# Products of k and v head by head in column tiles of 64, and loads issued at other steps of a span

## Chip, cores and metric

The kernel runs on one core of a Trainium2 chip. The metric is the device time of the whole launch in microseconds (us); the median of several runs is compared. The core has five engines that are told apart below: TensorE (PE, whose weight loads the profile lists apart as PEld), VectorE (DVE), ScalarE (ACT), GpSimd (POOL) and SyncE (SP). In this kernel POOL and SP mostly issue transfers, each through a queue of its own that is worked off in order.

## What is computed

Linear attention feeds a gated two-layer network. There are 8 batches, 8 heads, 576 positions and 64 dimensions per head, so 4608 tokens of width 512; the hidden width is 1536.

```python
q_s = exp(q - max(q, -1)); q_s /= sum(q_s, -1) + 1e-9
k_s = exp(k - max(k, 2));  k_s /= sum(k_s, 2) + 1e-9     # softmax over the positions
kv = einsum('bhsd,bhse->bhde', k_s, v)                   # 64 x 64 for each batch and head
x = einsum('bhsd,bhde->bhse', q_s, kv)                   # then (tokens, 512)
out = (sigmoid(x @ w_gate) * (x @ w_val)) @ w_out
```

## The kernel before

**Tiling.** Tokens are worked in nine windows of 512. Window 0 runs while the weights arrive and are prepared (the loop over j from 0 to 11, functions g1_0 and g2_0). From window 1 on each window is one span of six steps, at = 0 to 5, each over 256 of the 1536 hidden columns. A step is g1 (84 matmul passes, L696), h_split, side_a, g2 of the step before (48 passes, L768) and side_b. side_a(n, at) and side_b(n, at) prepare window n = w + 1 and batch n while window w multiplies: they are the attention part, cut into pieces p = 0 to 5 that go with the six steps.

**Products of k and v (k_mm, L381 to L392).** The 576 positions of a batch are five tiles: four of 128 rows and one of 64. Two heads (a pair, hp) stand side by side in 128 columns. For each tile and pair one matmul takes 128 columns of k as weights and 128 columns of v as the moving operand, so it computes four 64x64 blocks; the two on the diagonal are the two heads' products, the other two are not used. A batch has 20 matmuls into one PSUM tile named at. The data are float32, which TensorE works in two passes, so the profile shows 40 weight loads and 40 matmul records per batch. They are the step p = 2 of a span for batches 2 to 7, between g1 and g2; for batch 1 they stand in the first loop at j = 5, and batch 0 has a form of its own (k_mm_0).

**After the products (k_done, L410).** DVE scales the two diagonal blocks by the reciprocal sums with one instruction for each half of the partitions (diag_put, L398) into kmax_b, and kv_split makes a high and a low part for the second product (x_mm, L560).

**Loads (load_next, L839).** While window n is prepared, load_next(n, p) issues on SP what batch n + 1 needs: kT (k transposed, tiles kt, two 288 KB loads at p = 1 and two at p = 3), and at p = 5 four q tiles (ring<-qn_in), five k tiles (ring<-k_in) and five v tiles (v and f_last), 256 KB each, the last of k and v 128 KB. It stands at the end of side_b. Other SP transfers of a span are the maxima and sums of q to DRAM and back (q_m_row, q_r_row, then eight spread loads each into q_b, L491), q transposed (ring<-qT_in, L498) at p = 1, and the results (out). The four combined weights of the next step (s_sb, L288, 512 KB each) and the second-layer weights (wo_hl, L238) are reloaded in every step on POOL's queue; a reload is issued when the matmuls that read the tile are done, and the tile is read again one step later.

Of the kernel before, what the change touches and what calls it, by code (L numbers as in the profile page):

```python
# [8 lines left out]
F32 = mybir.dt.float32  # L9
# [5 lines left out]
ALU = mybir.AluOpType  # L15
AX = mybir.AxisListType

P = 128
B, H, S, D = 8, 8, 576, 64
# [6 lines left out]
NP = H // 2  # L26
# [4 lines left out]
NC = 4  # L31
# [20 lines left out]
def attn_moe(ctx: ExitStack, tc: tile.TileContext, qf, qn, qT, k, kT, v, wg, wv, wo, out):  # L52
    nc = tc.nc
# [23 lines left out]
    ps_at = ctx.enter_context(tc.tile_pool(name="ps_at", bufs=1, space=bass.MemoryType.PSUM))  # L77
# [14 lines left out]
        out=kv_sb.rearrange("p b i h e -> p (b i h e)"),  # L92
# [204 lines left out]
    kvps = {}  # L297
# [6 lines left out]
    def kT_load(b, hp, t=None):  # L304
        if t is None:
            t = kt_two[hp % 2]
            nc.sync.dma_start(out=t, in_=kT[b, hp * P:(hp + 1) * P])
        kT_sb[b, hp] = t

    def k_max(b, hp):  # L310
        if hp == 0:
            kmax[b], kneg[b], ksum[b] = (
                small.tile([P, NP], F32, name=f"k_{x}") for x in ("max", "neg", "sum")
            )
        m = kmax[b][:, hp:hp + 1]
        nc.vector.tensor_reduce(out=m, in_=kT_sb[b, hp], axis=AX.X, op=ALU.max)
        nc.vector.tensor_scalar(
            out=kneg[b][:, hp:hp + 1], in0=m, scalar1=-1.0, scalar2=None, op0=ALU.mult
        )

    def k_sum(b, hp):
        t = kT_sb.pop((b, hp))
        nc.scalar.activation(
            t, t, AF.Exp, bias=kneg[b][:, hp:hp + 1], accum_out=ksum[b][:, hp:hp + 1]
        )
# [11 lines left out]
    def k_load(b, t, kt=None):  # L337
        s0, n = KTILES[t]
        if kt is None:
            kt = ring.tile([P, DM], F32, name="ring")  # L340
        nc.sync.dma_start(out=kt[:n], in_=k[b, s0:s0 + n])
        kt_sb[b, t] = kt

    def v_load(b, t, vt=None):
        s0, n = KTILES[t]
        if vt is None:

            if t < 2:
                vt = v_two[t]
            else:  # L350
                vt = f_last[:, t - 2].rearrange("p n e -> p (n e)")
        v_sb[b, t] = vt
        src = v[b, s0:s0 + n]
        if b == 0:
            nc.sync.dma_start(out=vt[:n, :, 0:P], in_=src.rearrange("s (h e) -> s h e", e=P))
        else:
            nc.sync.dma_start(out=vt[:n], in_=src)
# [23 lines left out]
    def k_mm(b, t):  # L381
        n = KTILES[t][1]
        kt, vt = kt_sb[b, t], v_sb[b, t]
        if t == 0:
            kvps[b] = ps_at.tile([P, NP, P], F32, name="at")
        for hp in range(NP):
            sl = slice(hp * P, (hp + 1) * P)
            nc.tensor.matmul(  # L388
                kvps[b][:, hp], lhsT=kt[:n, sl], rhs=vt[:n, sl],
                start=(t == 0 and hp == 0), stop=(t == len(KTILES) - 1 and hp == NP - 1),  # L390
                skip_group_check=True,
            )  # L392

    def diag_put(o, ps, k_r, h0, h1):

        for a in range(2):
            sl = slice(a * D, (a + 1) * D)
            nc.vector.tensor_tensor(  # L398
                out=o(sl), in0=ps[sl, :, sl],
                in1=k_r[sl, h0:h1].unsqueeze(2).broadcast_to([D, h1 - h0, D]), op=ALU.mult,  # L400
            )
# [8 lines left out]
    def k_done(b):  # L410
        k_r = ksum.pop(b)
        nc.vector.tensor_scalar_add(k_r, k_r, EPS)
        nc.vector.reciprocal(k_r, k_r)
        kv = kmax_b[:, 0:NP * D].rearrange("p (h e) -> p h e", e=D)
        diag_put(lambda sl: kv[sl], kvps.pop(b), k_r, 0, NP)
        kv_32[b] = lambda sl: kv[sl]

    kv_32 = {}
# [24 lines left out]
    def qn_load(w, c):  # L443
        t = ring.tile([P, T], F32, name="ring")
        nc.sync.dma_start(out=t, in_=qf[w, c] if w < NF else qn[w - NF, c])
        qn_sb[w, c] = t.rearrange("p (i d) -> p i d", d=D)
# [41 lines left out]
    def q_spread(w, what, hp):  # L488
        q_b[w, what, hp] = t = four.tile([P, T], F32, name="q_b")
        for a in range(2):  # L490
            nc.sync.dma_start(  # L491
                out=t[a * D:(a + 1) * D],
                in_=q_row[w, what][2 * hp + a].unsqueeze(0).broadcast_to([D, T]),
            )

    def qT_load(w, hp):
        qT_sb[w, hp] = t = ring.tile([P, T], F32, name="ring")
        nc.sync.dma_start(out=t, in_=qT[w - NF, hp])  # L498
# [20 lines left out]
    def qT_mul(w, hp, eng=nc.vector):  # L519
        t = qT_sb[w, hp]  # L520
        eng.tensor_tensor(out=t, in0=t, in1=q_b.pop((w, "r", hp)), op=ALU.mult)
# [19 lines left out]
    def x_mm(w, hp):  # L541
        qh, ql = qT_hl.pop((w, hp))
        if w > 1 and hp < 3:
            ps = ps_gv.tile([P, T], F32, name="gv")
        else:
            ps = ps_at.tile([P, T], F32, name="at")
        x_ps[w, hp] = ps
        parts = x_parts(w)
        if len(parts) == 1 and hp == NP - 1:
            parts = [(parts[0][0], f, f + HT) for f in range(0, T, HT)]  # L550
        if w > 1 and hp == NP - 1:
            parts.sort(key=lambda x: (P <= x[2] - x[1] <= HT, x[2] - x[1]))
        for b, f, t in parts:
            kh, kl = (kv_sb[:, b % 2, i, hp] for i in range(2))
            for lh, rh in ((0, qh), (0, ql), (1, qh)):
                cuts = [f, t]
                if w > 1 and hp == NP - 1 and lh and t == parts[-1][2] and t - f > HT:
                    cuts.insert(1, (f + t) // 2)
                for f0, t0 in zip(cuts, cuts[1:]):
                    nc.tensor.matmul(  # L560
                        ps[:, f0:t0], lhsT=kl if lh else kh, rhs=rh[:, f0:t0],
                        start=(lh == 0 and rh is qh), stop=(lh == 1),
                        skip_group_check=True,
                    )

    def x_ev(w, hp):
        copy = nc.vector.tensor_copy if hp % 2 and w > 1 else nc.scalar.copy
        copy(out=x_32[:, hp], in_=x_ps.pop((w, hp)))
# [30 lines left out]
    def c_subs():  # L599

        def sub(i, x, y):
            c_32[i] = t = ring.tile([P, 2, HT], F32, name="ring")
            nc.vector.tensor_tensor(out=t, in0=x, in1=y, op=ALU.subtract)

        sub(T1, quarter(0, 1), quarter(0, 0))
        sub(T2, quarter(1, 1), c_32[T1])
        sub(T3, quarter(1, 1), quarter(0, 1))
        sub(T4, quarter(1, 0), c_32[T2])
# [209 lines left out]

    def side_b(n, p):
        if p == 0:  # L820
            for hp in range(NP):
                q_spread(n, "m", hp)
        if p == 1:
            for hp in range(NP):
                qT_load(n, hp)
        if p == 2:
            for hp in range(NP):
                q_spread(n, "r", hp)
        if p == 3:
            for hp in range(NP):  # L830
                qT_mul(n, hp)
        if p == 4:
            for hp in range(NP):
                x_mm(n, hp)
                x_ev(n, hp)
            c_subs()
        load_next(n, p)

    def load_next(n, p, vs=range(5)):  # L839

        if n + 1 >= NW:
            return
        b = n + 1 if n + 1 < B else None
        if b is not None:
            if p == 1:
                kT_load(b, 0); kT_load(b, 1)
            if p == 2:
                k_max(b, 0); k_max(b, 1)
            if p == 3:
                k_sum(b, 0); k_sum(b, 1)  # L850
                kT_load(b, 2); kT_load(b, 3)
            if p == 4:
                k_max(b, 2); k_max(b, 3)
                k_max_send(b)
                if b > 2:
                    k_max_read(b)
        if p == 5:
            for c in range(NC):
                qn_load(n + 1, c)
            if b is not None:  # L860
                for t in range(5):
                    k_load(b, t)
                for t in vs:
                    v_load(b, t)

# [71 lines left out]
    for t in range(0, 4, 2):  # L939
        rows = k[0, t * P:(t + 2) * P].rearrange("(t p) e -> p t e", p=P)  # L940
# [14 lines left out]
    for g in range(2):  # L955
        rows = kT[1, 2 * g * P:2 * (g + 1) * P].rearrange("(g p) s -> p g s", p=P)
# [23 lines left out]
    for t in range(2, 5):  # L980
        n = KTILES[t][1]
        nc.vector.tensor_tensor(out=top[:n], in0=top[:n], in1=kt_sb[0, t][:n], op=ALU.max)
    ps = ps_acc.tile([P, DM], F32, name="acc")
    for hp in range(NP):
# [6 lines left out]
        out=m, in_=ps.rearrange("p (h s) -> p h s", s=P), axis=AX.X, op=ALU.max  # L991
    )
    nc.vector.tensor_tensor(
        out=diag.rearrange("p (h s) -> p h s", s=P),
        in0=ident.unsqueeze(1).broadcast_to([P, NP, P]),
        in1=m.broadcast_to([P, NP, P]), op=ALU.mult,
# [105 lines left out]
    j, p = NJ - 1, NS - 1  # L1102
# [25 lines left out]
    for w in range(1, NW):  # L1128
        last = w == NW - 1
        for at in range(NS):  # L1130
            p = step(w, at)
# [61 lines left out]
```

## Time and profile before

| | |
|---|---|
| runs | 948.31, 948.54, 952.85 us; median 948.54 |
| profiled execution | 952.18 us, of which the profile's span is 950.2 us |
| PE busy in the span | 931.5 us, 7218 matmul records |
| DVE, ACT, POOL busy | 614.2, 487.7, 176.4 us |
| mean granted TensorE clock | 0.990 of 2.4 GHz |
| moved by DMA | 257.94 MB, mean 271 GB/s |

Busy time alone doesn't say what bounds the end: matmuls are pipelined, so PE counts as busy when it waits between two passes too. The rows further down are read by the distance between starts and by the waits.

### The profile page before, as it was taken

Reading aid. Unit: us, or ns where it says so; the run is one execution under the profiler, and the core shown is the slowest. Engines: PE = TensorE matmul, PEld = TensorE weight load, DVE = VectorE, ACT = ScalarE, POOL = GpSimd, SP = SyncE. Lnnn points to the kernel's source line nnn. Section 1 sums busy time; section 2 is a strip of 40 time slices with the busy share of each in tenths; the row PEclk is TensorE's granted clock in tenths of the full one; section 3 lists DMA queues with packets and bytes.
Section 4 is the critical chain, followed back from the end, with each engine's and each line's share of the span. In section 5 each row is a group of like instructions: output and inputs, shape, how many; then the busy total and the mean of one; then the engine's idle time right before and its main releaser. Section 6 shows DMA issues by size and latency. Waiting matters only on the chain.

```text
span 950.2 us, 18015 instructions
## 1 busy us (share of the span) xinstructions
PE 931.5 (98%) x7218; PEld 853.9 (90%) x7218; DVE 614.2 (65%) x1014; ACT 487.7 (51%) x824; POOL 176.4 (19%) x334
## 2 busy tenths in 40 slices
PE   5999899999999999999999999999999999999998
PEld 4644544799999999999999999999999999999998
DVE  7698879876566666656675668466755755564242
ACT  4589887564456345635472647264635343543222
POOL 0110112321122112211221222121212122212220
PEclk8899999999999999999999999999999999999999
DMA  9967686999699979998899979997999689858672
GB/s 315 346 221 287 217 299 199 365 361 298 206 264 361 295 233 249 371 293 270 210 379 301 275 167 382 325 285 153 382 321 260 213 248 324 249 179 264 204 218 69
DMA packets 96610, 257.94 MB, mean 271 GB/s; under 512 B 15568, under 2 KB 18128, under 8 KB 96528
## 3 DMA queue, kind: packets, MB, share of 16 engines
q0 software_dynamic: 46304, 168.32, 58.6%
q1 hardware_dynamic: 50224, 88.48, 32.1%
q8 instruction: 57, 0.93, 0.4%
q14 instruction: 25, 0.20, 0.1%
HBM read 228.20 MB, written 28.56 MB: 270 GB/s over the span
## 4 chain that ended last, share of the span: by engine, by line
PE 82%; issue 8%; DVE 4%; DMA 2%; POOL 1%; ACT 1%; SPq 0%; POOLq 0%; ACTq 0%; DVEq 0%
PE gv L696 48%; PE acc L768 28%; PE at L388 3%; PE gv L560 2%; DMA wo_raw<-wo_in 1%; POOL s L281 1%; DMA s<-s_sb 1%; DMA lent<-k_in 1%; PE at L560 1%; DVE s_sb L276 1%; DVE a_w L276 0%; POOL wo L229 0%; DVE c_hl L624 0%; PE acc L584 0%; PE gv L644 0%
## 5 line engine op out<-in xcount | busy, mean ns | idle before, releaser
L696 PE MATMUL gv<-c_hl,s_sb 128*128 128x256 f32 x2304 | 277.2, 276 | 0.0
L768 PE MATMUL acc<-wo_hl,h 128*128 128x256 f32 x2304 | 269.5, 276 | 0.0
L696 PEld LDWEIGHTS gv<-c_hl,s_sb 128*128 128x128 f32 x2304 | 268.6, 188 | 0.1
L768 PEld LDWEIGHTS acc<-wo_hl,h 128*128 128x128 f32 x2304 | 264.7, 188 | 0.7
L696 PE MATMUL gv<-c_hl,a_w 128*128 128x256 f32 x1728 | 220.6, 277 | 0.7 <-DVE h L656 0.7
L696 PEld LDWEIGHTS gv<-c_hl,a_w 128*128 128x128 f32 x1728 | 206.9, 188 | 1.8 <-DVE h L656 0.9
L288 POOL DMA_DIRECT2D s_sb<-s x188 | 99.6, 530 | 302.3 <-PE gv L696 300.3
L722 DVE TENSOR_TENSOR sg<-gv,sg 128x512 f32<-128x512 f32 x48 | 33.2, 691 | 134.7 <-PE gv L696 134.5
L238 POOL DMA_DIRECT2D wo_hl<-wo x96 | 50.9, 530 | 295.6 <-PE acc L768 293.2
L714 ACT COPY sg<-gv 128x512 f32<-128x512 f32 x48 | 28.2, 588 | 143.7 <-PE gv L696 143.0
L724 ACT COPY sg<-gv 128x512 f32<-128x512 f32 x48 | 28.2, 587 | 103.3 <-PE gv L696 103.3
L644 PE MATMUL gv<-x,f_w 128*128 128x512 f32 x160 | 72.2, 605 | 2.8 <-DVE h L656 2.8
L726 DVE TENSOR_TENSOR sg<-sg 128x512 f32<-128x512 f32 x48 | 33.2, 692 | 53.9 <-ACT sg L724 53.9
L644 PEld LDWEIGHTS gv<-x,f_w 128*128 128x128 f32 x160 | 30.6, 194 | 40.5 <-issue 35.8
L747 DVE TENSOR_TENSOR h<-sg,h 128x1024 fp32r<-128x1024 f32 x48 | 58.8, 1226 | 1.6
L735 DVE TENSOR_TENSOR sg<-sg 128x512 f32<-128x512 f32 x48 | 33.2, 692 | 33.6 <-ACT sg L729 33.6
L729 ACT ACTIVATE sg<-sg 128x512 f32<-128x512 f32 x48 | 30.4, 634 | 46.2 <-DVE sg L728 46.2
L719 ACT COPY sg<-gv 128x512 f32<-128x512 f32 x48 | 28.2, 587 | 37.2 <-PE gv L696 37.2
L716 ACT COPY sg<-gv 128x512 f32<-128x512 f32 x48 | 28.2, 587 | 36.7 <-PE gv L696 36.7
L678 PE MATMUL acc<-wo_t,h 128*128 128x512 f32 x96 | 43.1, 592 | 0.0
L502 DVE TENSOR_TENSOR ring<-ring,q_b 128x512 f32<-128x512 f32 x28 | 18.5, 691 | 37.8 <-DMA ring<-qT_in 37.6
L678 PEld LDWEIGHTS acc<-wo_t,h 128*128 128x128 f32 x96 | 18.2, 190 | 22.7 <-issue 21.3
(154 smaller groups left out, 1066.6 us busy)
## 6 DMA issues: line engine op xcount, KB each, us to landing
s_sb<-s POOLq DMA_DIRECT2D x188, 512.0 KB, 8.1
wo_hl<-wo POOLq DMA_DIRECT2D x96, 512.0 KB, 6.4
s<-s_sb POOLq DMA_DIRECT2D x24, 512.0 KB, 5.6
out<-x SPq DMA_DIRECT2D x35, 256.0 KB, 9.6
ring<-k_in SPq DMA_DIRECT2D x28, 256.0 KB, 14.7
ring<-qn_in SPq DMA_DIRECT2D x28, 256.0 KB, 10.4
q_b<-q_m_row SPq DMA_DIRECT2D x56, 128.0 KB, 9.7
ring<-qT_in SPq DMA_DIRECT2D x28, 256.0 KB, 6.9
```

The source lines that it names most:

```text
L238: nc.gpsimd.dma_start(out=t.rearrange("p h e -> p (h e)"), in_=wo_dram[2 * p + i].bitcast(F32R))
L288: nc.gpsimd.dma_start(out=s_sb[:, i].rearrange("p h n e -> p (h n e)"), in_=s_dram[p][:, i * n:(i + 1) * n].bitcast(F32R),)
L388: nc.tensor.matmul(kvps[b][:, hp], lhsT=kt[:n, sl], rhs=vt[:n, sl], start=(t == 0 and hp == 0), stop=(t == len(KTILES) - 1 and hp == NP - ...
L644: nc.tensor.matmul(ps[n], lhsT=w[:, kt // 2, sl], rhs=x_0[:, kt], start=(kt == 0), stop=(kt == NK - 1),)
L678: nc.tensor.matmul(acc[0][m], lhsT=h_0[j][:, m * P:(m + 1) * P], rhs=wo_t[j // 2][:, j % 2], start=(j == 0), stop=(j == NJ - 1),)
L696: nc.tensor.matmul(ps[:, n], lhsT=lh(kt), rhs=c_hl[i][:, x, kt], start=(first and n == 0 and kt == 0 and lh is wh and x == 0), stop=(last ...
L722: nc.vector.tensor_tensor(out=sg[:, 0], in0=rr, in1=sg[:, 0], op=ALU.add)
L726: nc.vector.tensor_tensor(out=sg[:, 3], in0=sg[:, 3], in1=sg[:, 2], op=ALU.add)
L729: nc.scalar.activation(sg[:, 0:2, 0], sg[:, 0:2, 0], AF.Sigmoid)
L735: tt(out=sg[:, 0:2, 0], in0=sg[:, 0:2, 0], in1=sg[:, 0:2, 1], op=ALU.mult)
L747: nc.vector.tensor_tensor(out=lo, in0=sg[:, :, 0], in1=hi.bitcast(F32), op=ALU.subtract)
L768: nc.tensor.matmul(acc[w][m][:, es], lhsT=h[lh][:, i, sl], rhs=o[i][:, rh, es], start=(at == 0 and i == 0 and lh == 0 and rh == 0 and e == 0),
```

## The change

Three things change. First, k_mm issues one matmul per head rather than per pair: 64 columns of k as weights, 64 columns of v moving, and the result goes to PSUM partitions 0 to 63 for even heads and 64 to 127 for odd heads. The program then carries a tile size of 128 x 64 (rows x columns of the array), or 64 x 64 for the last tile, at column 0 or 64. A batch has 40 matmuls, 80 passes. Second, k_done scales all of it with one DVE instruction of 128 partitions. Third, load_next issues kT of the first two pairs at p = 0, ahead of the spread of q's maxima; v at p = 2; q and three k tiles at p = 4; the other two k tiles at p = 5. For n = 1, in the first loop, all loads stay where they were.

```diff
 def k_mm(b, t):
-            kvps[b] = ps_at.tile([P, NP, P], F32, name="at")
-        for hp in range(NP):
-            sl = slice(hp * P, (hp + 1) * P)
+            kvps[b] = ps_at.tile([P, NP, D], F32, name="at")
+        for h in range(H):
+            hp, a = divmod(h, 2)
+            sl = slice(h * D, (h + 1) * D)
             nc.tensor.matmul(
-                kvps[b][:, hp], lhsT=kt[:n, sl], rhs=vt[:n, sl],
+                kvps[b][a * D:(a + 1) * D, hp], lhsT=kt[:n, sl], rhs=vt[:n, sl],
...
 def k_done(b):
-        diag_put(lambda sl: kv[sl], kvps.pop(b), k_r, 0, NP)
+        nc.vector.tensor_tensor(
+            out=kv, in0=kvps.pop(b), in1=k_r.unsqueeze(2).broadcast_to([P, NP, D]), op=ALU.mult
+        )
...
 def side_b(n, p):
         if p == 0:
+            load_next(n, 1)
             for hp in range(NP):
                 q_spread(n, "m", hp)
...
-        load_next(n, p)
+        if p > 1:
+            load_next(n, p)

 def load_next(n, p, vs=range(5)):
+        first = n == 1
+        def rows(t0, t1):
+            if t0 == 0:
+                for c in range(NC):
+                    qn_load(n + 1, c)
+            if b is not None:
+                for t in range(t0, t1):
+                    k_load(b, t)
...
+        if p == 2 and b is not None:
+            if not first:
+                for t in vs:
+                    v_load(b, t)
+            k_max(b, 0); k_max(b, 1)
...
+        if p == 4:
+            if not first:
+                rows(0, 3)
...
         if p == 5:
-            for c in range(NC):
-                qn_load(n + 1, c)
-            if b is not None:
-                for t in range(5):
-                    k_load(b, t)
+            if first:
+                rows(0, 5)
                 for t in vs:
                     v_load(b, t)
+            else:
+                rows(3, 5)
```

On PE, at step p = 2 of the span that prepares window 2, the kernel before has this row of instructions; a shape is that of the output, v_112, v_113 and f_last hold tiles of v, ring holds k.

```order
L696 MATMUL gv<-c_hl,a_w 128x256 x12
L388 MATMUL at<-v_112,ring 128x128 x4
L388 MATMUL at<-v_113,ring 128x128 x4
L388 MATMUL at<-f_last,ring 128x128 x12
L768 MATMUL acc<-wo_hl,h 128x256 x48
```

The changed kernel has this at the same place.

```order
L699 MATMUL gv<-c_hl,a_w 128x256 x12
L389 MATMUL at<-v_112,ring 64x64 x8
L389 MATMUL at<-v_113,ring 64x64 x8
L389 MATMUL at<-f_last,ring 64x64 x24
L771 MATMUL acc<-wo_hl,h 128x256 x48
```

Nothing stands elsewhere; 20 matmuls have become 40 of a quarter of the output each.

On SP's queue, from the end of one span's loads to p = 2 of the next (window 2 again), the kernel before has this; q_m_row and q_r_row are the rows in DRAM, kt_114 and kt_115 the two kT tiles.

```order
L451 DMA q_m_row<-q_m 128x32
L671 DMA out<-x_109 128x512 x4
L491 DMA q_b<-q_m_row 64x512 x8
L451 DMA q_r_row<-q_r 128x32
L498 DMA ring<-qT_in 128x512 x4
L307 DMA kt_114<-kT_in 128x576
L307 DMA kt_115<-kT_in 128x576
L491 DMA q_b<-q_r_row 64x512 x8
```

The changed kernel has this.

```order
L454 DMA q_m_row<-q_m 128x32
L674 DMA out<-x_109 128x512 x4
L307 DMA kt_114<-kT_in 128x576
L307 DMA kt_115<-kT_in 128x576
L494 DMA q_b<-q_m_row 64x512 x8
L454 DMA q_r_row<-q_r 128x32
L501 DMA ring<-qT_in 128x512 x4
L494 DMA q_b<-q_r_row 64x512 x8
L357 DMA v_112<-v_in 128x512
L357 DMA v_113<-v_in 128x512
L357 DMA f_last<-v_in 128x512 x2
L357 DMA f_last<-v_in 64x512
```

The two kT loads have moved ahead of the spread of the maxima, and the five v loads, which came behind k at p = 5, now follow the spread of the sums at p = 2.

## Rows read from the trace of the kernel before

**Rows 1.** Stretches: length, busy PE, PEld, DVE, ACT, POOL (count), clock, DMA, GB/s.
```profile
171.00:950.20 779.20, 774.77 (x6746) 770.07 (x6744) 473.87 (x776) 359.38 (x648) 153.19 (x289) 1.00 0.94 272
...
30.00:171.00 141.00, 138.23 (x387) 67.30 (x387) 116.81 (x203) 117.03 (x161) 19.32 (x35) 0.99 0.75 257
```

**Rows 2.** All waits of PE from 171 us on: total us, times, longest.
```profile
PE gv L696 <- DVE h L656: 0.7, 1, 0.7
```

**Rows 3.** PE in order of time at batches 2 and 7: start, length, group, count.
```profile
209.04 1.52 PE L696 MATMUL gv<-c_hl,a_w 128*128 128x256 f32 x12
210.41 1.95 PE L388 MATMUL at<-v,ring 128*128 128x128 f32 x16
212.19 3.04 PE L388 MATMUL at<-f_last,ring 128*128 128x128 f32 x24
215.16 2.10 PE L768 MATMUL acc<-wo_hl,h 128*128 128x256 f32 x16
...
699.56 1.95 PE L388 MATMUL at<-v,ring 128*128 128x128 f32 x16
...
704.31 2.89 PE L768 MATMUL acc<-wo_hl,h 128*128 128x256 f32 x23
```

**Rows 4.** L388's durations (ns, least, median, most), then its change to 64 rows and back.
```profile
L388 PE MATMUL at<-f_last,ring x160: 272/275/373, 97.6 to 704.1; 128*128 128x128 f32 x104, 64*128 64x128 f32 x56
...
213.53 0.91 PE L388 MATMUL at<-f_last,ring 128*128 128x128 f32 x5
...
214.07 0.48 PE L388 MATMUL at<-f_last,ring 64*128 64x128 f32 x2
...
215.16 0.51 PE L768 MATMUL acc<-wo_hl,h 128*128 128x256 f32 x2
```

**Rows 5.** Narrow windows: weight loads and matmuls with few moving columns.
```profile
149.90 0.53 PEld L560 LDWEIGHTS at<-ring,kv_sb 128*128 128x128 f32 x4 [0.24 <-DVE a_w L276]
...
250.64 0.33 PE L560 MATMUL gv<-ring,kv_sb 128*128 128x128 f32 x2
```

**Rows 6.** PE behind the products of batch 1, and the clock there.
```profile
111.49 3.60 PE L644 MATMUL gv<-x,f_w 128*128 128x512 f32 x8
117.86 5.40 PE L644 MATMUL gv<-x,f_w 128*128 128x512 f32 x8 [2.77 <-DVE h L656]
...
119.20:122.60 3.40, 3.40 (x5) 1.35 (x4) 3.37 (x7) 2.80 (x6) 0.00 (x0) 0.50 0.41 105
```

**Rows 7.** DVE and ACT from batch 1's products to that wait.
```profile
104.18 0.88 DVE L398 TENSOR_TENSOR kmax_b<-at,k_sum 64x256 f32<-64x256 f32 x2
...
104.63 0.86 ACT L425 CAST kv_sb<-kmax_b 64x256 fp32r<-64x256 f32 x2 [1.57 <-DVE kmax_b L398]
...
109.71 0.69 DVE L226 TENSOR_TENSOR wo_hl<-wo_t,wo_hl 128x512 fp32r<-128x512 f32 x1 [0.85 <-ACT wo_hl L222]
```

**Rows 8.** SP's queue at the start of the first span.
```profile
188.51 1.81 SPq L671 DMA_DIRECT2D out<-x  x4
194.84 8.41 SPq L491 DMA_DIRECT2D q_b<-q_m_row  x8
...
205.65 4.42 SPq L498 DMA_DIRECT2D ring<-qT_in  x4
```

**Rows 9.** The reload of the fourth combined weight, and the weight load that needs it.
```profile
194.42 0.54 POOL L288 DMA_DIRECT2D s_sb<-s  x1 [0.83 <-PE gv L696]
...
207.22 0.52 PEld L696 LDWEIGHTS gv<-c_hl,s_sb 128*128 128x128 f32 x2
```

**Rows 10.** Reloads of s_sb, issue to landing, issued in 186 to 201 and 231 to 246.
```profile
DMA to landing us min/median/max: 11.4/12.0/13.1
...
DMA to landing us min/median/max: 4.1/4.8/5.0
```

**Rows 11.** DVE behind the products of batch 4.
```profile
416.30 2.69 DVE L502 TENSOR_TENSOR ring<-ring,q_b 128x512 f32<-128x512 f32 x4 [6.49 <-DMA ring<-qT_in]
...
422.88 0.69 DVE L722 TENSOR_TENSOR sg<-gv,sg 128x512 f32<-128x512 f32 x1
```

More of the change, by code (lines that the diff above doesn't have):

```diff
@@ L843, in load_next @@
         b = n + 1 if n + 1 < B else None
-        if b is not None:
[L845 to L852, printed above, removed]
+        first = n == 1
[6 more added lines that the diff above has]
+                    k_load(b, t)
+        if p == 1 and b is not None:
+            kT_load(b, 0); kT_load(b, 1)
+        if p == 2 and b is not None:
[3 more added lines that the diff above has]
+            k_max(b, 0); k_max(b, 1)
+        if p == 3 and b is not None:
+            k_sum(b, 0); k_sum(b, 1)
+            kT_load(b, 2); kT_load(b, 3)
+        if p == 4:
+            if not first:
+                rows(0, 3)
+            if b is not None:
                 k_max(b, 2); k_max(b, 3)
@@ L857, in load_next @@
         if p == 5:
-            for c in range(NC):
-                qn_load(n + 1, c)
-            if b is not None:
-                for t in range(5):
-                    k_load(b, t)
+            if first:
+                rows(0, 5)
                 for t in vs:
                     v_load(b, t)
+            else:
+                rows(3, 5)
     def beside_first(j):
```

## The prediction, made before the changed kernel ran

> **What bounds the kernel now.** I read the busy time by stretch first. From 171 us to the end PE is busy for 774.77 of 779.20 us at a granted clock of 1.00 [rows 1], and all its waits in that stretch come to 0.7 us [rows 2]. So the last 82% of the span is one unbroken row of matmul passes. What leaves that row shortens the kernel by its full length; what moves on DVE, ACT, POOL or SP there costs nothing until it makes PE wait. Between 30 and 171 us PE is busy for 138.23 of 141 us [rows 1], with one long wait, 2.77 us for DVE [rows 6].
>
> Next, the length of one pass. In batch 2 sixteen passes of the k and v products start at 210.41 and the next group at 212.19 [rows 3]: 1.78 / 16 = 0.111 us per pass of 128 weight columns and 128 moving columns. The main matmuls with 256 moving columns take (210.41 - 209.04) / 12 = 0.114 [rows 3]. Weight loads whose matmuls have 64 moving columns follow each other at (0.53 - 0.19) / 3 = 0.113, taking 0.19 for a load [rows 5]. So for 64, 128 or 256 moving columns a pass costs about the same, and what they share is the loading of 128 weight columns. Two matmuls with 128 moving columns start 0.33 - 0.27 = 0.06 apart where weights are ready, 0.27 being the least duration of a matmul of that shape [rows 4, 5]: issue alone permits 0.06.
>
> Last, the changes of array shape. The five matmuls from 213.53 span 0.91, the last of them having 64 rows and taking 0.37, the longest of its line, so four distances make 0.54 where 4 x 0.111 = 0.44 is usual: 0.09 extra. The two 64-row matmuls from 214.07 are 0.48 - 0.27 = 0.21 apart, 0.10 extra [rows 4]. Entering a new shape costs 0.09 + 0.10 = 0.19. On the way back the first two passes of the second layer are 0.22 to 0.24 apart (0.51 less a duration of 0.27 to 0.29) [rows 4], 0.11 extra or a little more, and as much as 0.09 stands before them: about 0.20.
>
> **The change part by part: the products.** A batch costs 215.16 - 210.41 = 4.75 us [rows 3] plus the 0.11 behind it, 4.86. That is 40 x 0.111 = 4.45, two changes of shape (0.39), and rounding. There are six such batches in the unbroken row; rows 3 show the first and the last, 4.75 both times (704.31 - 699.56).
>
> The new form has 80 passes, each with half the weight columns and half the moving columns, and three changes of shape: into 128 x 64, into 64 x 64 and back, 3 x 0.195 = 0.59. What a half-width pass costs is in no row. A float32 pass of 512 moving columns takes (3.60 - 0.59) / 7 = 0.43 us [rows 6], so 128 columns stream in 0.107; of 0.111 only 0.004 is fixed, and half the columns would take 0.054 + 0.004 = 0.058. Three prices follow:
> - Two halves abreast: neighbouring heads use different columns of the array and different partitions of PSUM, so nothing that one waits for (its weights' slot, its columns) belongs to the other. 80 x 0.058 / 2 = 2.3, with the shapes 2.9, a gain of 1.95 per batch, 11.7 for six.
> - One after the other: 80 x 0.058 = 4.6, with the shapes 5.2, a loss of 0.4 per batch, 2.2 for six.
> - No cheaper than a full pass: 80 x 0.111 = 8.9, with the shapes 9.5, a loss of 4.6 per batch, 28 for six.
>
> I take the first. The rows speak for a price by columns: loads and streams of one pass already run beside each other, or a pass would take 0.107 twice and not 0.111, so TensorE does overlap whatever doesn't share a resource. Against it speaks that the two passes of one head follow each other on the same half, so the next head's load must be let past one that waits. If half of the overlap is lost, the gain is 6 instead of 11.7.
>
> On this point the Trainium skill is weighed too. Its page TensorEngine Tiling (Array Packing), section Key Properties, says that different tiles can load weights and multiply in parallel, which would give the first price; no row here shows two tiles at work at once, so it isn't confirmed.
>
> Batch 1 is different. Its products end before PE's 2.77 us wait for DVE [rows 6], so a gain there only lengthens that wait. DVE's chain to it gets one instruction for two of 0.88 us together [rows 7], some 0.4 less, but ACT's kv_split waits for the scaled products as before [rows 7], and DVE waits 0.85 us for ACT further on [rows 7]: I take 0, at best -0.4. The longer wait has a price of its own. Behind it the granted clock stood at 0.50 for 3.4 us with PE busy [rows 6]; another such stretch would cost 3.4 / 2 = 1.7. So 0 to +1.7 for that, taken as 0. In batches 2 to 7 the shorter scaling on DVE is covered: PE doesn't wait for it.
>
> **The loads.** The same bytes are moved, and PE waits for no load now, so the gain is 0 from this part alone; what remains is what they run into. The closest place is the first span. The reload of the fourth combined weight is issued at 194.42, and the load that needs it comes about 0.22 late at 207.4 (two loads span 0.52 where 0.19 + 0.11 is usual) [rows 9]: it lands just in time, 13.0 us after its issue. Reloads of that stretch take 11.4 to 13.1 [rows 10]. SP there waits from the results at 188.51 + 1.81 until 194.84 for the maxima to come back [rows 8], and the two kT loads, 2 x 288 KB, now go into that gap. At the 272 GB/s of rows 1 they take 2.2 us; the reloads land up to that much later, and PE waits 0 to 2.2 once. I take 0.7, since the reloads share the engines with everything else. The spread loads behind kT lose nothing: they wait for the maxima until 194.84 anyway. The out transfers ahead of kT wait for ACT's copies, which stand behind the k_sum that frees the kT tiles, so kT itself adds no wait on SP.
>
> The v loads at p = 2 queue behind the spread of the sums; behind them on SP are the kT loads of p = 3, whose readers come at the end of p = 4. At that step reloads take 4.1 to 5.0 us [rows 10], far under 13.0, so 1.2 MB more has room. The q and three k loads at p = 4 wait for PE's x_mm to free ring buffers, and behind them on SP is the sending of k's maxima, which waits for DVE behind x_mm anyway. DVE waits 6.49 us for q transposed in front of its scaling, and reaches the next evacuation at 422.88 [rows 11]; kT ahead of these loads adds at most 2.2 there, and v gone from p = 5 takes more off. PE doesn't wait for that evacuation until its PSUM buffer comes round in the next step, some 10 us later. I cost all this at 0.
>
> **Sum.** -11.7 for six batches, 0 for batch 1, +0.7 for the first span: -11.0. The profiled execution took 952.18 us (span 950.2), so 941.2, a ratio of 0.9885. It is above the median of 948.54 by 0.4%; on the median the forecast is 948.54 x 0.9885 = 937.6.
>
> **The rivals.**
> - The halves take turns. For it speaks the order within a head (two passes on the same half), and that no row shows two tiles abreast; against it, that pass time here goes with what is shared. Six batches +2.2, first span +0.7: 948.54 x (952.18 + 2.9) / 952.18 = 951.4, within 0.5%. Here belongs a pace of issue: at the 0.06 between starts of rows 5 a batch takes 80 x 0.06 + 0.59 = 5.4, six +3.2, and the end is 952.4. The Trainium skill, TensorE: Matmul & The Clock Gate, section "Wait — 56ns, not 53.3ns?", gives about 62 ns per matmul where the sequencer decodes them itself; by that the end would be about 953.3 (an estimate).
> - A half pass costs as much as a whole one. This is the slower end, and one mechanism: a price per weight load that doesn't go with its columns. For it: 64 rows instead of 128 don't shorten a pass, since 212.19 to 215.16 with 8 of 24 passes at 64 rows [rows 3] is 24 x 0.111 and the shape costs. Against it: rows are not columns. Six batches +28; batch 1 adds 4.6 - 2.77 = +1.8, as the wait swallows the rest; with +0.7 the end is 978.9. It decides against the old kernel from a half pass of (4.86 - 0.59) / 80 = 0.053 on, and costs over 0.5% from about 0.063 on.
> - The halves run abreast, but the moved loads stall PE: reloads of s_sb that land later than 13.0 us after issue. v at p = 2 and q and k at p = 4 meet them in five spans (n = 2 to 6). At 2.2 us per span, the price of the kT loads above, that is +11, and the end is 948.5. Against it: the 4.1 to 5.0 of rows 10.
>
> **How the numbers follow.** Halves abreast 0.52 (935 to 943, from a pass cost without its fixed part to half of the overlap); turns or pace 0.30 (949 to 953); no cheaper pass 0.10 (960 to 980); abreast with stalls 0.08 (943 to 949). About 0.5%, 4.7 us, is what a measurement of this kernel can tell from no change. Faster by more than that is the first case, 0.52; within it are the second and the fourth, 0.38; slower 0.10. The range has to take in the second case: 934.5 to 952.5 leaves out the third and the edges.
>
> **What would show it.** In the changed trace the products of batch 2, from their first matmul to the first of the second layer, take 2.9 us (abreast), 5.2 (turns) or 9.5 (no cheaper), and starts of neighbouring heads' passes lie under 0.03 apart or at 0.058. PE's wait for DVE near 115 us grows from 2.77 to about 4.7 if abreast, and shrinks if not. PE's waits behind 171 us stay near 0.7, plus up to 2.2 at the first span's fourth combined weight. Any longer wait of PE for s_sb there makes the part on loads wrong; a product time over 4.86 makes the forecast wrong in sign.

## The result and the profile after

The changed kernel took 939.38 us (937.87 to 941.41), beside 949.67 us for the kernel before on the same chip: a ratio of 0.9888, 95% interval 0.9853 to 0.9923. The forecast was 937.6 us in a range of 934.5 to 952.5, and faster by over 0.5% as the likeliest case. On another chip, further below, the ratio was 0.9906 (0.9877 to 0.9934). The profiled execution took 938.32 us with a span of 936.5; the one of the kernel before, 952.18 with 950.2. Times are medians of all executions, while ratios compare executions in the same state, so that of e1 below leaves out its two slowest of twelve (963.92 and 970.60 us).

The stretches of the changed kernel come first, with the columns of rows 1, then all waits of PE from 171 us on, as in rows 2.

```profile
171.00:936.50 765.50, 760.59 (x6975) 756.06 (x6973) 468.26 (x767) 358.22 (x646) 152.68 (x288) 1.00 0.96 276
117.20:120.60 3.40, 3.40 (x6) 1.42 (x5) 3.37 (x7) 2.77 (x6) 0.00 (x0) 0.53 0.41 92
```

```profile
PE gv L699 <- DVE h L659: 0.7, 1, 0.7
```

PE is still busy to the end, and its busy time behind 171 us fell from 774.77 [rows 1] to 760.59. It waits no more than before [rows 2]. So the gain shows as work that left PE's row; the experiments tell what let it through.

Where it left shows in PE's order of time at batches 2 and 7, to be held against rows 3.

```profile
207.13 1.52 PE L699 MATMUL gv<-c_hl,a_w 128*128 128x256 f32 x12
208.59 1.15 PE L389 MATMUL at<-v,ring 128*64 128x64 f32 x32
209.57 1.72 PE L389 MATMUL at<-f_last,ring 128*64 128x64 f32 x48
211.21 2.31 PE L771 MATMUL acc<-wo_hl,h 128*128 128x256 f32 x18
...
687.51 1.15 PE L389 MATMUL at<-v,ring 128*64 128x64 f32 x32
...
690.13 2.08 PE L771 MATMUL acc<-wo_hl,h 128*128 128x256 f32 x16
```

The products take 211.21 - 208.59 = 2.62 us, where they took 4.75 [rows 3]. From batch 2 to batch 7 the starts lie 687.51 - 208.59 = 478.92 apart, where it was 699.56 - 210.41 = 489.15 [rows 3]: five batches gave 10.23, 2.05 each. The whole account of the spans is: 1.82 up to the products of batch 2, 10.23 between, and 1.65 behind (batch 7's own 2.05, less a remainder of 0.40), together 13.7 = 950.2 - 936.5. The 1.82 at the front is mostly scatter: in the second run of the changed kernel (e11, further below) these products start at 210.73, later than in the kernel before.

How the passes run is seen from the durations of L389 (ns, least, median, most) and then from narrow windows in order of time, where a row holds the records that reach into the window.

```profile
L389 PE MATMUL at<-v,ring x224: 222/222/270, 93.6 to 688.4; 128*64 128x64 f32 x112
```

```profile
208.59 0.28 PE L389 MATMUL at<-v,ring 128*64 128x64 f32 x2
...
208.69 0.58 PE L389 MATMUL at<-v,ring 128*64 128x64 f32 x14
```

The first two passes span 0.28 together, and each of them takes 0.27, the most of its line: they start within 0.01 us of each other, so they run abreast. The third pass starts at 208.69 and the 33rd, the first of f_last, at 209.57: thirty passes in 0.88 us, 0.029 a pass or 0.058 for a pair of halves. So neighbouring heads run abreast, each on its own half of the columns. The Trainium skill, page TensorEngine Tiling (Array Packing), section Key Properties, says that tiles load weights and multiply in parallel; the rows of the changed kernel agree.

Batch 1 went much as told. DVE's scaling is one instruction of 0.42 instead of two over 0.88 [rows 7], and then it waits for ACT; PE's wait for DVE grew from 2.77 [rows 6] to 3.81, with 0.47 for ACT beside it; the low clock, near 1.2 of 2.4 GHz, stayed one stretch of 3.4 us (0.53 above, 0.50 in rows 6).

```profile
102.58 0.42 DVE L416 TENSOR_TENSOR kmax_b<-at,k_sum 128x256 f32<-128x256 f32 x1
...
103.47 0.87 DVE L429 TENSOR_TENSOR kv_sb<-kmax_b,kv_sb 64x256 fp32r<-64x256 f32 x2 [0.47 <-ACT kv_sb L428]
...
108.60 3.70 PE L647 MATMUL gv<-x,f_w 128*128 128x512 f32 x8 [0.47 <-ACT h L655]
116.12 5.40 PE L647 MATMUL gv<-x,f_w 128*128 128x512 f32 x8 [3.81 <-DVE h L659]
```

### The profile page after: what moved, and what is told of

It reads as the page before. It is cut to its first block, busy times and chain, and to the rows that moved or that the text cites. A ratio compares the mean times of both kernels' runs of the same rounds, so it can differ in the third digit from the quotient of the medians.

```text
span 936.5 us, 18595 instructions
## 1 busy us (share of the span) xinstructions
PE 914.0 (98%) x7498; PEld 835.8 (89%) x7498; DVE 609.7 (65%) x1007; ACT 488.0 (52%) x824; POOL 176.4 (19%) x334
## 4 chain that ended last, share of the span: by engine, by line
PE 83%; DMA 5%; DVE 5%; ACT 4%; issue 1%; SPq 1%; POOL 0%; ACTq 0%; DVEq 0%
PE gv L699 48%; PE acc L771 28%; PE gv L563 2%; PE at L389 2%; PE gv L647 1%; DMA kmax_row<-k_max 1%; DMA ring<-qf_in 1%; PE acc L681 1%; DMA sg<-wg_in 1%; DVE s_sb L276 1%; DMA wo<-wo_hl 1%; PE at L563 1%; DVE s L250 1%; DVE a_w L276 1%; DMA lent<-k_in 1%
## 5 line engine op out<-in xcount | busy, mean ns | idle before, releaser
L725 DVE TENSOR_TENSOR sg<-gv,sg 128x512 f32<-128x512 f32 x48 | 33.2, 692 | 152.3 <-PE gv L699 152.3
L717 ACT COPY sg<-gv 128x512 f32<-128x512 f32 x48 | 28.2, 588 | 130.8 <-PE gv L699 130.2
L732 ACT ACTIVATE sg<-sg 128x512 f32<-128x512 f32 x48 | 30.4, 634 | 46.0 <-DVE sg L731 46.0
L719 ACT COPY sg<-gv 128x512 f32<-128x512 f32 x48 | 28.2, 587 | 36.8 <-PE gv L699 36.8
L731 DVE TENSOR_TENSOR sg<-gv,sg 128x512 f32<-128x512 f32 x48 | 33.2, 692 | 2.3
```

The source lines that it names most:

```text
L725: nc.vector.tensor_tensor(out=sg[:, 0], in0=rr, in1=sg[:, 0], op=ALU.add)
L731: nc.vector.tensor_tensor(out=sg[:, 1], in0=z, in1=sg[:, 1], op=ALU.add)
L732: nc.scalar.activation(sg[:, 0:2, 0], sg[:, 0:2, 0], AF.Sigmoid)
```

## The experiments

The theory put to the test: the halves abreast are the whole gain, and the moved loads are worth nothing. The first rival: the loads have a part in it. All ratios are to the kernel before, run beside it on the same chip.

**The products alone, and the loads alone.** e1 has the new products and scaling with the loads of the kernel before:

```diff
 def side_b(n, p):
         if p == 0:
-            load_next(n, 1)
...
-        if p > 1:
-            load_next(n, p)
+        load_next(n, p)
...
 def load_next(n, p, vs=range(5)):
...
         if p == 5:
-            if first:
-                rows(0, 5)
+            for c in range(NC):
+                qn_load(n + 1, c)
+            if b is not None:
+                for t in range(5):
+                    k_load(b, t)
                 for t in vs:
                     v_load(b, t)
-            else:
-                rows(3, 5)
```

> The kernel before with the new k_mm and the new scaling, all loads where they were. Theory (the products alone make the gain, since the halves run abreast and PE waits for no load): products of batch 2 take 2.63 us as in the changed kernel, the span is 12 to 13 us shorter than before, ratio to before 0.987 to 0.990, the same as the changed kernel within 1.5 us. Rival (the moved loads carry a share, because a shorter row of passes would run into reloads of s_sb that the old order of loads makes late): the gain is at least 2 us smaller than that of the changed kernel, and PE shows waits for s_sb behind 171 us that add up to that.

e2 has the reverse, the moved loads with the products of pairs:

```diff
 def k_mm(b, t):
-            kvps[b] = ps_at.tile([P, NP, D], F32, name="at")
-        for h in range(H):
-            hp, a = divmod(h, 2)
-            sl = slice(h * D, (h + 1) * D)
+            kvps[b] = ps_at.tile([P, NP, P], F32, name="at")
+        for hp in range(NP):
+            sl = slice(hp * P, (hp + 1) * P)
...
 def k_done(b):
-        nc.vector.tensor_tensor(
-            out=kv, in0=kvps.pop(b), in1=k_r.unsqueeze(2).broadcast_to([P, NP, D]), op=ALU.mult
-        )
+        diag_put(lambda sl: kv[sl], kvps.pop(b), k_r, 0, NP)
```

> The kernel before with the moved loads alone; products and scaling as before. Theory: ratio to before 0.999 to 1.002; products 4.75 us each, PE waits behind 171 us stay near 0.7 us, and DVE's waits for q transposed and for the q rows change without any effect on PE. Rival (the loads help or harm on their own): over 2 us either way, seen as PE's waits for s_sb or for DVE.

e1 took 957.04 us, ratio 1.0016 (0.9983 to 1.0049); e2 took 952.96, ratio 1.000 (0.9981 to 1.0018). Neither half gains anything; together they gain 1%. Products and scaling were changed together in e1 and e2; the scaling alone was not run. Yet the products of e1 take 2.63 us a batch as in the changed kernel. The time comes back as waits. The rival had the sign right and the place wrong: of PE's waits from 171 us on in e1 only 0.3 us is for s_sb. Beside the 0.7 us for DVE that stands in the kernel before too, the rest is for ACT:

```profile
PE gv L699 <- ACT sg L717: 11.7, 4, 4.4
...
PE gv L699 <- DMA s_sb<-s: 0.3, 1, 0.3
```

The chain that makes one of them: the start of the products of batch 2 first, then, in order of time behind the products of batch 3, DVE, ACT and PE of e1.

```profile
209.15 1.15 PE L389 MATMUL at<-v,ring 128*64 128x64 f32 x32
...
315.06 1.29 DVE L505 TENSOR_TENSOR ring<-ring,q_b 128x512 f32<-128x512 f32 x2 [6.40 <-DMA ring<-qT_in]
317.66 1.38 DVE L505 TENSOR_TENSOR ring<-ring,q_b 128x512 f32<-128x512 f32 x2 [1.31 <-DMA kt<-kT_in]
...
323.60 0.69 DVE L725 TENSOR_TENSOR sg<-gv,sg 128x512 f32<-128x512 f32 x1
...
325.53 0.63 ACT L732 ACTIVATE sg<-sg 128x512 f32<-128x512 f32 x1 [4.59 <-DVE sg L731]
...
332.39 0.56 ACT L717 COPY sg<-gv 128x512 f32<-128x512 f32 x1
...
333.00 1.64 PE L699 MATMUL gv<-c_hl,s_sb 128*128 128x256 f32 x12 [1.80 <-ACT sg L717]
```

DVE waits for q transposed, no longer than the 6.51 us of the kernel before at this place, and then for kT. It comes late to the evacuation at L725, so ACT's activation at L732 waits 4.59 us for it. Behind that activation ACT has the split of k and v, a table load, the exponentials of q and the sums of k without a break, and then the copy L717 that frees the PSUM buffer that PE wants. In the kernel before, the same places read, with the row of PE last:

```profile
324.93 0.69 DVE L722 TENSOR_TENSOR sg<-gv,sg 128x512 f32<-128x512 f32 x1
...
327.88 0.64 ACT L729 ACTIVATE sg<-sg 128x512 f32<-128x512 f32 x1 [1.50 <-DVE sg L728]
...
335.31 0.59 ACT L714 COPY sg<-gv 128x512 f32<-128x512 f32 x1 [0.47 <-PE gv L696]
...
335.11 2.88 PE L696 MATMUL gv<-c_hl,s_sb 128*128 128x256 f32 x24
```

ACT reaches the copy only 0.47 us before PE has filled the buffer. The copy ends at 335.31 + 0.59 = 335.90, and PE writes that buffer again with the last twelve of these 24 passes, from 335.11 + 12 x 0.113 = 336.47 on, 0.57 later. So this end of the chain has 0.47 + 0.57 = 1.0 us of slack. DVE was just in time as well. In e1, where DVE is the last, the activation starts 325.53 - 323.60 = 1.93 after DVE's evacuation; here it starts 2.95 after it, so DVE had 1.0 to give. Together that is 2.0, about what one batch of short products takes from PE's row. The chain paced by the loads doesn't come forward: counted from the first product of batch 2, DVE's evacuation stands at 324.93 - 210.41 = 114.52 before and at 323.60 - 209.15 = 114.45 in e1, while PE's next step, which starts at 333.75 before and 328.31 in e1, has come forward by 4.2, two batches' worth. After two batches the slack is gone. In the changed kernel the same places show DVE waiting for PE again, and the 0.47 of ACT is back:

```profile
318.50 0.69 DVE L725 TENSOR_TENSOR sg<-gv,sg 128x512 f32<-128x512 f32 x1 [2.06 <-PE gv L699]
...
321.87 0.63 ACT L732 ACTIVATE sg<-sg 128x512 f32<-128x512 f32 x1 [1.50 <-DVE sg L731]
...
329.31 0.59 ACT L717 COPY sg<-gv 128x512 f32<-128x512 f32 x1 [0.47 <-PE gv L699]
```

Waits for ACT explain 11.7 of the 21.4 us between the spans of e1 (957.9) and the changed kernel (936.5). The trace of e1 is one of its slower executions: it took 959.89 us beside the median of 957.04, and the fastest took 949.30. A further part is the clock behind the two longest waits (windows of e1):

```profile
433.60:440.40 6.80, 5.60 (x26) 5.60 (x27) 1.15 (x3) 2.21 (x5) 0.53 (x1) 0.50 0.60 189
...
638.40:641.80 3.40, 3.40 (x18) 3.40 (x17) 0.38 (x2) 0.58 (x1) 0.53 (x1) 0.50 0.63 210
```

PE stood idle 4.36 and 3.81 us before them. At 0.50, 1.2 of 2.4 GHz, the 26 passes of the first stretch take 5.60 / 26 = 0.215 us each instead of 0.113, about twice as long, so 5.60 and 3.40 us of busy time cost 4.5 us. Some 4 us more are a slow rhythm that e3 below shows better: counted by the starts in the trace of e1, 943 passes 117.7 ns apart instead of 113.3.

**Which of the moved loads does it.** Three kernels with the new products, each with a part of the moves. e7 moves kT alone (e1 with this):

```diff
 def side_b(n, p):
         if p == 0:
+            load_next(n, 1)
...
-        load_next(n, p)
+        if p > 1:
+            load_next(n, p)
```

> New products with the loads of v, q and k at their old step; only the first two transposed k loads go to the head of a span. Theory (the crowd of loads of v, q and k at the last step holds up the transposed q, and with it the chain VectorE, ScalarE, TensorE): the transposed q still lands late, VectorE still waits 5 to 7 us for it in the span of batch 3, only the 1.3 and 0.7 us for transposed k go; TensorE still waits 5 to 12 us in all for ScalarE behind 171 us, ratio to the kernel before 0.996 to 1.003. Rival (the order of transposed k and transposed q is what counts): TensorE's wait for ScalarE is under 1 us and the ratio is near 0.989.

e8 moves v, q and k and leaves kT (the changed kernel with the inverse of that diff).

> The changed kernel with the first two transposed k loads back at their old step; v, q and k are loaded at the changed steps. Theory (the crowd at the last step): VectorE's wait for transposed q falls from 6.4 to under 1 us in the span of batch 3, ScalarE reaches its first copy of the next step before TensorE is done, TensorE waits under 1.5 us in all behind 171 us, ratio 0.987 to 0.993. Rival (the order of transposed k): VectorE waits for transposed k instead, TensorE waits 4 us or more for ScalarE, ratio 0.996 to 1.002.

e10 moves v alone (e1 with this):

```diff
 def load_next(n, p, vs=range(5)):
             if p == 2:
+                if n != 1:
+                    for t in vs:
+                        v_load(b, t)
                 k_max(b, 0); k_max(b, 1)
...
         if p == 5:
...
-                for t in vs:
-                    v_load(b, t)
+                if n == 1:
+                    for t in vs:
+                        v_load(b, t)
```

> New products; of the loads only v is moved, from the last step of a span to the third step of it; q, k and transposed k stay. Theory (the crowd): five of the last step's loads, some two fifths of its bytes, are gone from ahead of transposed q; VectorE's wait for it falls from 6.4 to 2 to 4 us, and TensorE's waits for ScalarE from 11.7 to 0 to 4 us in all; ratio 0.988 to 0.995. Rival (q and k alone still make transposed q late): TensorE waits 8 us or more for ScalarE, ratio 0.997 to 1.003.

Measured: e7 974.92 us, ratio 1.0225 (1.0175 to 1.0275); e8 942.22, 0.9898 (0.9861 to 0.9936); e10 942.21, 0.9897 (0.9859 to 0.9935). Moving v alone lets the whole gain through; moving kT alone makes it about 2% slower than the kernel before. The ratios of e8 and e10 lie in the ranges expected of the theory. DVE's first wait for q transposed at the same place, with ACT's activation behind it, in e7 and then in e10; behind them all waits of PE from 171 us on in e10:

```profile
321.38 0.69 DVE L505 TENSOR_TENSOR ring<-ring,q_b 128x512 f32<-128x512 f32 x1 [10.89 <-DMA ring<-qT_in]
...
333.35 0.63 ACT L732 ACTIVATE sg<-sg 128x512 f32<-128x512 f32 x1 [10.59 <-DVE sg L731]
```

```profile
312.18 0.69 DVE L505 TENSOR_TENSOR ring<-ring,q_b 128x512 f32<-128x512 f32 x1 [1.45 <-DMA ring<-qT_in]
...
324.51 0.64 ACT L732 ACTIVATE sg<-sg 128x512 f32<-128x512 f32 x1 [1.50 <-DVE sg L731]
```

```profile
PE gv L699 <- DVE h L659: 0.8, 1, 0.8
PE gv L699 <- DMA s_sb<-s: 0.7, 1, 0.7
```

e1 had 6.40 there. The crowd of q, k and v at the last step of a span stands ahead of q transposed; taking v's 1.2 MB out shortens the wait by 4.95 us, and those bytes at the 272 GB/s of rows 1 are 4.4 us. Putting kT into that crowd, ahead of q transposed, lengthens it by 4.49, more than the 2.2 us of its bytes. The expectation for e7 was wrong: I reckoned with what kT gains for its own readers and not with what it takes from q transposed. PE's waits for ACT came to 15.1 us there, where 5 to 12 were expected. In the changed kernel, where v, q and k have moved, kT's early place does no harm. What q and k add to v's move doesn't show in the time, as e8 and e10 agree within their intervals. It shows in DVE: between 200 and 720 us its waits for q transposed come to 37.6 us before, 41.7 in e1, 16.9 in e10 and 3.1 in e8, and in the changed kernel, with kT early, to 17.1. So q and k take off most of what v leaves, and PE has no use for it. Moving q or k alone was not tried.

**What the pair abreast hangs on.** e3 is the changed kernel with all even heads of a tile before the odd ones:

```diff
-        for h in range(H):
+        for h in (0, 2, 4, 6, 1, 3, 5, 7):
```

> The changed kernel with the heads of a tile in the order 0, 2, 4, 6, 1, 3, 5, 7, so that neighbouring matmuls use the same half of the array in 3 of 4 cases; same work, same number of passes, same loads. Theory (the gain is two halves abreast; a half pass alone costs 0.058 us): passes of one half follow each other at 0.058 us; if the queue lets nothing past, one tile takes 16 x 0.058 = 0.93 less a little overlap at the two seams, the products of a batch about 4.6 to 5.2 us, and the time is within 3 us of the kernel before. Rival 1 (the gain comes from smaller passes, not from neighbours abreast): products 2.6 us as in the changed kernel. Rival 2 (TensorE looks far ahead and pairs passes that stand 8 apart): also about 2.6 to 3 us.

It took 955.62 us, ratio 1.0024 (1.0005 to 1.0043). The products of batch 2, on PE:

```profile
211.21 1.37 PE L389 MATMUL at<-v,ring 128*64 128x64 f32 x29
212.36 0.27 PE L389 MATMUL at<-f_last,ring 128*64 128x64 f32 x1
212.41 0.22 PE L389 MATMUL at<-v,ring 128*64 128x64 f32 x1
...
214.73 1.44 PE L771 MATMUL acc<-wo_hl,h 128*128 128x256 f32 x10
```

They take 3.52 us: between the 2.62 of the pair abreast and the 5.2 of turns. A pass of the next tile's even heads (f_last, 212.36) starts before one of the last odd heads of this tile (v, 212.41): passes of a free half are let past some that wait; how far ahead, these rows don't settle. The expected time, within 3 us of the kernel before, came true by luck, since the products took less than expected. They take 1.2 us less per batch than the 4.75 of the kernel before, PE waits no more than it did there, and yet the time is that of the kernel before. What takes it back is the pace of the passes behind the products. Ten microseconds behind them in e3, and then in the changed kernel, in the columns of rows 1, each with the next unbroken group of 48 passes:

```profile
216.00:226.00 10.00, 10.00 (x87) 10.00 (x86) 4.89 (x11) 1.76 (x3) 2.13 (x4) 1.00 1.11 330
...
230.38 5.82 PE L771 MATMUL acc<-wo_hl,h 128*128 128x256 f32 x48
```

```profile
212.00:222.00 10.00, 10.00 (x91) 10.00 (x90) 3.68 (x9) 1.76 (x3) 2.12 (x4) 1.00 1.18 343
...
226.28 5.60 PE L771 MATMUL acc<-wo_hl,h 128*128 128x256 f32 x48
```

87 passes stand against 91, at a granted clock of 1.00 in both. From one start to the next it is (5.82 - 0.28) / 47 = 0.118 us instead of (5.60 - 0.28) / 47 = 0.113, counted by the starts 117.7 ns instead of 113.3, for some 312 passes behind each batch, until x_mm. That costs 312 x 4.4 ns = 1.4 us, 8.2 for six batches, more than the shorter products give (7.4).

e9 takes the even heads first in four tiles and alternates in the last:

```diff
+        order = range(H) if t == len(KTILES) - 1 else (0, 2, 4, 6, 1, 3, 5, 7)
-        for h in range(H):
+        for h in order:
```

> The changed kernel, with the heads taken even then odd in the first four tiles of a batch and alternating only in the last tile. Theory (the slow rhythm of 117.7 ns behind the products depends on how the last passes end): products take 3.3 to 3.4 us a batch, the 312 passes behind them start 113 to 114 ns apart, and the time is 4 to 6 us above the changed kernel's: ratio 0.992 to 0.996. Rival (the rhythm comes from what went before, not from the last passes): products 3.3 to 3.4 us, 312 passes behind them 117 to 118 ns apart, ratio 1.000 to 1.003.

It took 946.97 us, ratio 0.9932 (0.9907 to 0.9956), with 91 passes in the ten microseconds behind its products of 3.23 us:

```profile
206.42 1.37 PE L390 MATMUL at<-v,ring 128*64 128x64 f32 x29
...
209.65 0.61 PE L772 MATMUL acc<-wo_hl,h 128*128 128x256 f32 x3
```

```profile
212.00:222.00 10.00, 10.00 (x91) 10.00 (x89) 4.21 (x10) 1.76 (x3) 2.13 (x4) 1.00 1.05 329
```

Behind all six batches e9 has 91 passes in ten microseconds where e3 has 87. So how the last tile's passes end decides the rhythm behind the products. It is not the only thing that does: stretches of 298 passes at 117.7 ns stand elsewhere too, once in e9 (from 558 us) and twice in e8 (from 466 and 564), whose heads alternate in every tile. What in the array the rhythm is, the rows don't say.

**Tiles of 32, and the changed kernel again.** e5 cuts each head into two column tiles of 32:

```diff
-            nc.tensor.matmul(
-                kvps[b][a * D:(a + 1) * D, hp], lhsT=kt[:n, sl], rhs=vt[:n, sl],
+            for i in range(2):
+                o, c = a * D + i * 32, h * D + i * 32
+                nc.tensor.matmul(
+                    kvps[b][o:o + 32, hp], lhsT=kt[:n, c:c + 32], rhs=vt[:n, sl],
```

> The changed kernel, each head's product cut once more into two column tiles of 32, so 160 passes a batch instead of 80, in four column positions. Theory (passes in different columns run alongside each other as far as columns go, 58 ns for a pass in its own): four abreast, 5 x 4 x 58 ns = 1.16 us of passes and some 0.2 to 0.4 us of shape changes, so 1.2 to 1.6 us a batch; TensorE then outruns ScalarE, whose slack is 0.5 us a span, so of the 6 x 1.2 = 7 us some come back as waits: ratio to the changed kernel 0.993 to 1.000, to the kernel before 0.982 to 0.990. Rival (a pair abreast is bound by the issue of one pass each 29 ns): 160 x 0.029 = 4.6 us a batch, near the 4.75 of the kernel before, ratio to the changed kernel 1.010 to 1.014.

> The changed kernel once more, on the chip of the run with tiles of 32. Ratio to the kernel before 0.985 to 0.992 as in its first comparison; products 2.63 us a batch; TensorE waits about 0.7 us behind 171 us.

e5 took 952.80 us, ratio 1.0007 (0.9983 to 1.0032), and the changed kernel beside it 942.64, 0.9906 (0.9877 to 0.9934). The products of batch 2 in e5, the longest stop within those of batch 4, and its longest waits:

```profile
209.57 1.10 PE L391 MATMUL at<-v,ring 128*32 128x64 f32 x64
...
212.07 4.48 PE L773 MATMUL acc<-wo_hl,h 128*128 128x256 f32 x37
...
410.76 0.52 PE L391 MATMUL at<-f_last,ring 64*32 64x64 f32 x19 [2.87 <-issue]
```

```profile
PE at L391 <- issue: 3.9, 3, 2.9
PE acc L773 <- issue: 2.8, 2, 1.7
```

Four tiles do run abreast: 64 passes in 1.10 us, (1.10 - 0.22) / 63 = 0.014 a pass, half of the 0.029 above. But a product is two passes, which my 1.16 us forgot, and each takes 4 x 0.014 = 0.056 in its own columns, as long as with 64: the weight columns were halved, the 64 moving columns were not. So the products take 212.07 - 209.57 = 2.50 us, 0.12 less than with 64. The rival was wrong as well, since issue goes far below 29 ns; that the ratio to the changed kernel, 952.80 / 942.64 = 1.011, lies in its range is luck. The 10 us lost lie in five stops for "issue", 6.7 us in all, within or soon after the products, where PE waits for nothing that the profile names, and in slow passes behind two batches. That PE's instructions arrive too late when twice as many are used up is only argued.

**Tiles of even length.** e6 cuts the 576 rows of k and v of batches 1 to 7 into five nearly equal tiles, to spare the change to 64 rows:

```diff
+KROWS = [(0, 116), (116, 115), (231, 115), (346, 115), (461, 115)]
...
+    def k_tile(b, t):
+        return KROWS[t] if b else KTILES[t]
...
-        s0, n = KTILES[t]
+        s0, n = k_tile(b, t)
```

> The changed kernel with the 576 positions of batches 1 to 7 cut into rows of 116, 115, 115, 115, 115 instead of four times 128 and once 64, so that no tile needs the 64 x 64 shape. Theory (a change of shape costs about 0.2 us, and the rows of a tile don't change a pass): 80 passes in 2.3 us, products of a batch 2.45 us instead of 2.63, six batches 1.1 us less in all; the time is 0.5 to 1.5 us below the changed kernel, hardly above the noise, so the trace decides. Rival (the step in the products comes from the wait for the last v tile, not from the shape): products stay at 2.6 us.

It took 1006.66 us, ratio 1.057 (1.0536 to 1.0605). The products are down by 0.15 us a batch, about one change of shape, but waits that the expectation left out ruin it. PE's three largest behind 171 us in e6:

```profile
PE gv L703 <- ACT sg L721: 21.1, 5, 6.0
PE gv L703 <- DVE sg L729: 8.9, 3, 5.1
PE gv L703 <- DMA s_sb<-s: 6.8, 8, 2.0
```

The Trainium skill, page DMA: Bandwidth & Descriptors, section "Why a DMA increments its semaphore by 16 and not by 1", says that a transfer uses the largest number of engines up to 16 that divides the slowest dimension of both its sides. By that rule, an estimate, it would be 5 for 115 rows and 4 for 116, where 128 and 64 use 16. The waits agree in direction; how many engines moved each load no row here shows, so the cause of the waits is not shown. They are 36.8 of the 73.1 us between the spans (1009.6 and 936.5); the mean granted clock is lower too, 0.965 against 0.993.

## Why the prediction came out, and where it was wrong

- **The products** were right in mechanism and close in size. A batch with its changes of shape went from 4.86 to about 2.81 (the distance between batches fell by 2.05), where the prediction had 2.9 and a gain of 1.95. The half pass of 0.058 is 0.058 as measured.
- **The changes of shape**, taken at three times 0.195, are within about 0.1 us of that per batch; the sum with the passes was 2.9 against some 2.8.
- **Turns and pace of issue** fell. A pass follows every 29 ns, and in e5 every 14, so the 0.06 of rows 5 is no bound of issue. The 62 ns of the Trainium skill, page TensorE: Matmul & The Clock Gate, section "Wait — 56ns, not 53.3ns?", aren't seen here either.
- **No cheaper pass** fell: a half pass takes 0.058 in its own half. e5 adds which columns set that: with 32 weight columns and the same 64 moving ones it is still 0.056, so it is the streaming, from which the prediction had reckoned it, and not the loading of weights.
- **Batch 1** was taken at 0, with -0.4 at best: the wait grew by 1.04 plus 0.47 for ACT instead of the 1.9 given, so it came to about -0.4, and the clock added no stretch.
- **The first span**, +0.7 for kT ahead of the reloads, didn't come: PE waits there for no reload. An error of 0.7 in a sum of 11. Single waits of 0.3 to 0.8 for a reload do stand in e1, e2, e7, e8 and e10, one in each.
- **The loads** are the wrong step, and luck kept it out of the number. "PE waits for no load now, so the gain is 0 from this part alone" is true, as e2 shows. But the prediction then let the end of that wait lie "some 10 us" from PE: "PE doesn't wait for that evacuation until its PSUM buffer comes round in the next step". From DVE's late evacuation the chain goes through ACT's whole row of work to the copy L714 and the buffer that it frees. There the slack is 1.0 us, and DVE's own is 1.0: 2.0 in all, not 10. The terms -11.7 and 0 do not add: without the moved loads the first is 0 or less (e1), and with them it is what was forecast. The sum came out because the change held both, not because the prediction saw that it needed both. The rival that moved loads stall PE had the sign of their effect reversed.
- **The total.** Forecast ratio 0.9885, measured 0.9888 and 0.9906. By single profiled executions it was -13.9 us where -11.0 was reckoned, of which 1.4 to 1.8 is scatter at the front.

Still open: whether moving q or k alone would do as well as v, why the stops of e5 come, and what else sets the rhythm of the passes.

## What to carry to other kernels

When PE is the bound, shortening its work by 2 us per span also takes 2 us from the slack of every chain that feeds it and isn't paced by it: before counting the gain, follow such a chain through all engines, in the kernel before, to the wait at its end, and read how much slack there is on the way (here 1.0 us at ACT's copy and 1.0 at DVE). An edit that gains nothing alone can be what lets another one through, so test each alone and both together. When loads pile up at one step, look first at what stands behind them in the queue. Here taking out v, the last of them, was enough.

## What the runs showed of the hardware

- Column tiles run abreast two or four at a time: 29 ns a pass with 64 columns, 14 with 32. A pass takes 0.056 to 0.058 us in its own tile either way, with 64 moving columns in both.
- A row of passes keeps a rhythm of 113.3 or 117.7 ns, at full granted clock, from one disturbance to the next; 87 or 91 passes in ten microseconds. It made 8 us in e3, and behind the products the order of the heads in one small tile of each batch decided it.
- Twice as many, smaller passes in the products (e5, one trace) came with stops of up to 2.87 us for which the profile names no releaser.
